# Two weight blocks of w3 loaded and turned first, and the order of all work planned again (attention and feed-forward, one core)

## The chip, the core and the metric

The kernel runs on one core of a Trainium2 chip. The metric is the device time of one execution in microseconds. A core has a matrix engine (TensorE, in the profile PE, with its weight loads as PEld), a vector engine (VectorE, DVE), a scalar engine (ScalarE, ACT), a general engine (GpSimd, POOL) and a queue for transfers (SyncE, SP). Transfers are issued from SP, ACT and POOL; the loads that also convert float32 to bfloat16 are all issued from POOL.

## The reference

```python
def _attn_ref(q, k, v, g_q, g_k):          # 8 batches, 12 heads, 448 positions, 64 values a head
    q_n, k_n = (rmsnorm(q, g_q), rmsnorm(k, g_k))
    scores = scale * np.matmul(q_n, k_n.transpose(0, 1, 3, 2))
    attn = np.exp(scores - np.max(scores, axis=-1, keepdims=True))
    attn = attn / (np.sum(attn, axis=-1, keepdims=True) + 1e-09)
    return np.matmul(attn, v)

def _moe_ref(x, w1, w2, w3, w_out):        # x is (3584, 768): the attention's heads side by side
    a = x @ w1                             # w1, w2: (768, 1024)
    b = x @ w2
    h = a * b @ w3                         # w3: (1024, 1024)
    return h @ w_out                       # w_out: (1024, 768)
```

## The kernel before, in words

**Units.** The attention is cut into 24 units: a batch and four of its twelve heads. For each unit the kernel loads q and k (L380), squares them on ACT (L477), sums the squares on DVE (L484), takes the scale from a logarithm and an exponential on ACT (L493, L496) and multiplies on DVE (L507). The scaled values are turned (transposed) to `qkT`: by PE for the first five units (L1134, in `do_turn`, with a copy from PSUM at L365 or L371), by transposing transfers on SP for the others (L579, in `send`). Seven score passes follow for a unit (`do_score`, matmuls L690); each fills two PSUM banks and is emptied by one exponential on ACT (L712). When all seven are done and `v` has landed (L420), the values follow (`start_pv`: L777 for the main part, L756 for a rest that two units share, when two units are taken together). ACT makes the reciprocal of the sums (L799, L800), DVE multiplies by it and writes `xT` (L819).

**Feed-forward.** Because `(a*b) @ w3 @ w_out` equals `(a*b) @ (w3 @ w_out)`, the kernel first computes the product of w3 and w_out once. For that w3 is loaded in eight blocks of 128 rows (`load_w3`, L455) and w_out in four quarters (`load_wout`, L461). PE turns each w3 block (`do_w3_turn`, L1156), a copy writes it to `w3T`, and pairs of passes multiply it with w_out (`w34_pair`, run by `do_pass`, matmuls L879); the result is `w34s`. Then for each batch four pairs of products with w1 and four with w2 follow (`ffn1_pair`), DVE multiplies the two (L960), and tiles of the product go through `w34s` (`ffn2_pair`), are copied from PSUM and stored (L1016). All of these matmuls are at L879; the trace tells them apart by their tiles (`w3T`, `w1s`, `w2s`, `abT`). The last tile has its own code (`do_last`, L1075).

**Halves of the array.** A pass is four matmuls of 64 rows by 64 columns that run side by side. After half of a pair's sums the two row halves exchange their banks; the instruction after the exchange waits for a small waiting instruction on SP or POOL (`hand_over`, L863), which itself waits for PE.

**The order of work.** No engine finds its order at run time. While the program is built, a planner (`Planner`) keeps a clock, one expected duration for each kind of job, and a model of the transfers, and takes one job after the other in the order of its expected times. The constants at the head of the kernel function steer it: how many pairs are open at once (`PAIRS`), by how much PE's work is put after its inputs (`MARGINS`), when scores go ahead of feed-forward passes (`STARVES`, `HUNGERS`, `FULL`), which of the score turns are given up (`AGAINST`), how late transfers land (`LATE`) and so on. Loads on POOL are issued in the order of `POOL_ORDER`, in which o is a quarter of w_out, w a block of w3, a and b a third of w1 and w2, q the two loads of a unit's q and k, and v the four loads of a unit's v. Each issue on POOL waits until the load eight places before it has landed. Where the planner sees PE idle in the first microseconds it puts matmuls without a use (`do_warm`, L1204), after fifteen larger ones at the very beginning (L1331).

Of the kernel before, what the change touches and what calls it, by code (L numbers as in the profile page):

```python
# [19 lines left out]
INF = float("inf")  # L20
# [4 lines left out]
LAG = {"ACT": 0.11, "DVE": 0.09, "SP": 0.0, "POOL": 0.0}  # L25
AHEAD = {"SP": 2.0, "POOL": 1.6}
AFTER = 0.7
LATE = 0.581
BUSY = 75.0


# [14 lines left out]
class Planner:  # L46
# [50 lines left out]
    def commit(self, job, start, engine):  # L97
# [9 lines left out]
        if job.moves is not None:  # L107
# [4 lines left out]
            def landed(t):  # L112
                self.note(job, t, engine)
                t += LATE if t > BUSY else 0.0
                ticket[0] = t
# [80 lines left out]
def kernel(  # L196
# [40 lines left out]
    psum = ctx.enter_context(tc.tile_pool(name="ps", bufs=1, space=PSUM))  # L237

    N_PE_T = 5
    QUAD = 13.0  # L240
    WARM = 15
    WARM_TO = 13.0
    WARM_N = 256
    PAIRS = (2, 3)
    MARGINS = (0.25, 0.294)
    LOWS = (2, 2)
    VALUE_BANKS = (6, 6)
    HOLD = 1
    SOONS = (0, 0)
    STARVES = (4, 5)  # L250
    HUNGERS = (0.6, 0.461)
    ONES = (0, 0)
    FULL = (0.3, 0.247)
    PARTS = ((2, 4, 6, 8), (2, 4, 6, 8), (4, 8))
    EARLY_PAIRS = 3
    AHEAD_W3 = 4
    EARLY = 4
    STOCKS = (14, 14)
    PACES = (1.7, 1.774)
    SWITCH = 55.0  # L260
    LATER = 11.735
    BY_G = 0.36
    KEYS = (1.8, 1.725)
    AGAINST = (34, 49, 79, 99, 106, 116, 117, 134, 151, 166, 172, 176, 185, 190, 197, 219, 244, 250, 265, 270, 282, 289, 301, 307, 318, 327)
    POOL_ORDER = (
        "o0 w0 w1 w2 o1 o2 o3 q1 v0 w3 w4 q2 w5 a0 v1 w6 w7 v2 a1 v3 q3 a2 b0 b1 q4 q5 b2".split()
    )
    ON_POOL = (1, 2, 3, 4, 5)
    IN_PARTS = (6, 7, 8)
    FIRST = 3.5  # L270
    THIN_FROM = 8
    THIN = 1.2
    QUIET = 0.546

    w1s = const.tile([128, CM, DFF], BF, name="w1s")
    w2s = const.tile([128, CM, DFF], BF, name="w2s")
# [45 lines left out]
    plan = Planner()  # L322

    def phase():
        return int(plan.now >= SWITCH)

    def quad(i):
        return QUAD * min(i, 6) + LATER * max(i - 6, 0)

    free, add = plan.free, plan.add  # L330
# [16 lines left out]
    w_at = {"w3": [INF] * CF, "w3T": [INF] * CF, "w_out": [INF] * 4, "w1": [INF] * NQB, "w2": [INF] * NQB}  # L347
# [120 lines left out]
    def plan_prep(i):  # L468
# [53 lines left out]
        s["red_at"] = [INF, INF]  # L522
        s["sent"] = [INF, INF]
        scaled_x = [[], []]
        pieces = ((0, 1), (1, 2)) if i == 0 else ((0, 2),)

        def reduced(t):
            def done(z):
# [47 lines left out]
            return done  # L576

        def send(t):
            nc.sync.dma_start_transpose(  # L579
                out=s["qkT"][:, t], in_=s["qks"][:, t].rearrange("p j x d -> p (j x d)")  # L580
            )
# [146 lines left out]
    def pv_size(t):  # L728
# [7 lines left out]
        if pv_one(i + 1, t):  # L736
            return 2
        if next_score[0] >= (i + 2) * NU - SOONS[phase()]:
            return 0
        if i == 1:  # L740
            return 0
        stock = sum(p.name != "w" for p in waiting)
        return 1 if stock < LOWS[phase()] or all_of(w34_at, CF) > t else 0

# [85 lines left out]


    pairs = []
    waiting = []
    running = [None]

# [21 lines left out]
    def hand_over(p, mm, t):  # L857

        at = t + 0.23
        e = "POOL"  # L860
        if max(w_at["w2"]) == INF or free["SP"] <= at and plan.moving["POOL"]:
            e = "SP"
        nop = (nc.sync if e == "SP" else nc.gpsimd).nop()  # L863
        tc.add_manual_dep(
            nop.ins, mm.ins.name, SYNC_DEP, reason="first half of the sums complete"
        )
        free[e] = max(free[e], at)
        p.gap_at = free[e] + 0.15
        p.nop = nop
# [304 lines left out]
    def next_pair(t):  # L1174
        if len(pairs) >= (EARLY_PAIRS if w_at["w_out"][3] == INF else PAIRS[phase()]):
            return None
# [17 lines left out]
    def pe_step(t):  # L1194

        took = pe_try(t, t - MARGINS[phase()])
        took = pe_try(t, t) if took is None else took
        if took is None and t < WARM_TO and idle_banks(t):
            return do_warm(single(idle_banks(t)))
# [52 lines left out]
    def pe_try(t, r):  # L1252
# [9 lines left out]
        last = HOLD and pairs and not any(p.ready() <= r for p in waiting)  # L1262
        if size == 2 and len(idle) >= VALUE_BANKS[phase()] and not last:
            return start_pv(t, 2, idle)
# [159 lines left out]
```

## Time and profile before

| what | value |
|---|---|
| median of three runs | 351.48 us (350.93 to 351.58) |
| the profiled execution's own time | 351.21 us |
| its span in the profile | 349.4 us |
| PE busy | 342.1 us, 98% of the span |
| ACT busy | 264.1 us, 76% |
| DVE busy | 203.6 us, 58% |
| granted TensorE clock | 1.0 |

The span goes from the first to the last instruction; 1.81 us of the profiled execution's time lie outside it. Matmuls are pipelined, so the busy time of PE is not the time in which it does useful work. What PE loses is read from the distance between the starts of two passes that follow each other: a pass of 448 columns after another starts 0.189 us later, one of 384 columns 0.162 us later, and what is over that is a wait or a change of the array's shape.

### The profile page before, as it was taken

The page shows a single profiled execution, that of the slowest core. Times are in us where ns is not written, and L with a number is a line of the kernel's source. Part 1 is how long each engine was busy: PE and PEld are TensorE (multiplying, and loading weights), DVE is VectorE, ACT ScalarE, POOL GpSimd, SP SyncE. Part 2 cuts the span into 40 slices and gives each one's busy share as a digit, 9 for nine tenths or more (in the row PEclk, how much of TensorE's full clock was granted, in tenths as well). Part 3 has the DMA queues.
Part 4 walks back from the last instruction along what each step waited for, and adds up shares of the span by engine and source line. Part 5 has one row for each costly group of instructions (what it writes and reads, how often), then busy time and mean ns, then how long its engine had stood idle before and what let it go on. Part 6 is the DMA issues. An engine that isn't in the chain of part 4 may idle for free.

```text
span 349.4 us, 16159 instructions
## 1 busy us (share of the span) xinstructions
PE 342.1 (98%) x7373; PEld 216.6 (62%) x7373; DVE 203.6 (58%) x292; ACT 264.1 (76%) x375; POOL 77.0 (22%) x134
## 2 busy tenths in 40 slices
PE   8999999999999999999999999999999999999995
PEld 4766756666665766556656575566565656666674
DVE  5369377988859597479657985687513421222100
ACT  4769979979998999888899997787796872222122
POOL 8366820202221403221122032204311000000000
PEclk9999999999999999999999999999999999999999
DMA  8999999587996999967999999955971013200054
GB/s 195 235 279 186 236 289 253 131 181 154 201 219 206 164 186 223 172 201 146 169 218 244 172 172 188 252 148 71 167 111 21 4 47 82 59 4 2 4 171 149
DMA packets 68488, 55.11 MB, mean 158 GB/s; under 512 B 45060, under 2 KB 62372, under 8 KB 68420
## 3 DMA queue, kind: packets, MB, share of 16 engines
q1 hardware_dynamic: 49440, 35.33, 43.5%
q0 software_dynamic: 18048, 16.92, 28.6%
q10 hardware_dynamic: 932, 1.84, 1.4%
q8 instruction: 57, 0.93, 1.1%
q14 instruction: 11, 0.09, 0.1%
HBM read 46.66 MB, written 11.01 MB: 165 GB/s over the span
## 4 chain that ended last, share of the span: by engine, by line
PE 85%; ACT 5%; DMA 3%; DVE 3%; issue 2%; POOL 2%; POOLq 0%; DVEq 0%
PE ps_all L879 62%; PE ps_all L777 11%; PE ps_all L690 9%; DMA w_outs<-in_moe_w_out_dram 3%; ACT P L712 2%; PE ps_all L756 2%; ACT sq L477 1%; DVE qks L507 1%; PE ps_all L1075 1%; POOL w_outs L461 1%; DVE xT L819 1%; POOL w3s L455 0%; PE ps_all L1156 0%; DVE ssq L484 0%; DVE abT L960 0%
## 5 line engine op out<-in xcount | busy, mean ns | idle before, releaser
L712 ACT ACTIVATE P<-ps_all 128x896 bf16<-128x896 f32 x114 | 101.0, 917 | 9.7 <-PE ps_all L690 8.6
L420 POOL DMA_DIRECT2D v_sb<-in_v_dram x96 | 57.4, 614 | 179.3 <-PE ps_all L690 107.2
L879 PE MATMUL ps_all<-xT,w2s 64*64 64x448 bf16 x1536 | 88.5, 349 | 0.1
L879 PE MATMUL ps_all<-xT,w1s 64*64 64x448 bf16 x1536 | 87.8, 349 | 0.0
L879 PE MATMUL ps_all<-w34s,abT 64*64 64x384 bf16 x1728 | 78.5, 323 | 0.0
L365 ACT ACTIVATE half<-ps_all 128x768 f32<-128x768 f32 (+1 forms) x38 | 32.6, 862 | 49.0 <-PE ps_all L879 48.8
L960 DVE TENSOR_TENSOR abT<-ps_all,half 128x896 bf16<-128x896 f32 x32 | 34.9, 1089 | 54.4 <-PE ps_all L879 52.6
L879 PEld LDWEIGHTS <-abT 64*64 64x64 bf16 x1728 | 51.6, 107 | 19.6 <-issue 0.4
L484 DVE TENSOR_REDUCE ssq<-sq 128x14 f32<-128x896 f32 (+1 forms) x50 | 51.1, 1042 | 20.2 <-ACT sq L477 20.2
L879 PEld LDWEIGHTS <-w2s 64*64 64x64 bf16 x1536 | 45.6, 107 | 26.7 <-issue 0.3
L879 PEld LDWEIGHTS <-w1s 64*64 64x64 bf16 x1536 | 45.1, 107 | 26.8
L690 PE MATMUL ps_all<-qkT 64*64 64x448 bf16 x672 | 60.3, 351 | 0.7 <-DVE qkT L371 0.3
L507 DVE TENSOR_TENSOR qks<-qk_sb,al 128x448 bf16<-128x448 f32 x96 | 54.5, 618 | 4.3 <-ACT al L496 4.1
L477 ACT ACTIVATE sq<-qk_sb 128x896 f32<-128x896 f32 (+1 forms) x50 | 45.2, 916 | 0.4 <-DMA qk_sb<-in_q_dram 0.4
L819 DVE TENSOR_TENSOR xT<-ps_all,r 128x448 bf16<-128x448 f32 x48 | 27.5, 618 | 17.1 <-ACT r L800 14.7
L690 PEld LDWEIGHTS <-qkT 64*64 64x64 bf16 x672 | 20.8, 106 | 15.0 <-issue 4.7
L879 PE MATMUL ps_all<-w_outs,w3T 64*64 64x384 bf16 x512 | 25.1, 323 | 1.2 <-DVE w3T L371 0.5
L777 PE MATMUL ps_all<-P,v_sb 128*32 128x448 bf16 x456 | 25.0, 352 | 0.0
L712 ACT ACTIVATE w_outs<-ps_all 128x896 bf16<-128x896 f32 x24 | 21.4, 916 | 4.1 <-PE ps_all L690 3.8
L777 PEld LDWEIGHTS <-v_sb 128*32 128x32 bf16 x592 | 15.8, 97 | 12.2
L712 ACT ACTIVATE Pr<-ps_all 128x896 bf16<-128x896 f32 x24 | 22.0, 917 | 0.8 <-PE ps_all L690 0.7
L879 PEld LDWEIGHTS <-w3T 64*64 64x64 bf16 x512 | 15.3, 107 | 7.6 <-SPq L863 1.1
(62 smaller groups left out, 207.0 us busy)
## 6 DMA issues: line engine op xcount, KB each, us to landing
out_dram<-half SPq DMA_DIRECT2D x48, 192.0 KB, 3.3
qk_sb<-in_q_dram SPq DMA_DIRECT2D x15, 448.0 KB, 5.7
qk_sb<-in_k_dram SPq DMA_DIRECT2D x15, 448.0 KB, 5.4
v_sb<-in_v_dram POOLq DMA_DIRECT2D x48, 64.0 KB, 4.0
v_sb<-in_v_dram POOLq DMA_DIRECT2D x48, 48.0 KB, 4.3
qk_sb<-in_q_dram POOLq DMA_DIRECT2D x5, 448.0 KB, 11.1
qk_sb<-in_k_dram POOLq DMA_DIRECT2D x5, 448.0 KB, 12.6
w3s<-in_moe_w_dram POOLq DMA_DIRECT2D x8, 256.0 KB, 6.9
```

What stands on the lines that cost most here:

```text
L365: nc.scalar.activation(out=out, in_=in_, func=AF.Copy, scale=1.0 if by is None else by)
L420: nc.gpsimd.dma_start(out=v_bufs[i % 4][p0 : p0 + HP, g::2, 0 : j1 - j0].rearrange("p h j d -> p h (j d)"), in_=src[:, g::2, j0:j1].rearra ...
L477: nc.scalar.activation(out=s["sq", t][:, x0:x1], in_=src[:, t, x0:x1], func=AF.Square)
L484: nc.vector.tensor_reduce(out=s["ssq"][:, t, x0:x1], in_=s["sq", t][:, x0:x1], axis=AX, op=ADD)
L507: nc.vector.tensor_tensor(out=s["qks"][:, t, :, x], in0=src[:, t, x], in1=s["alpha"][:, t, x].unsqueeze(2).broadcast_to([NP, NJ, D]), op=MULT,
L690: nc.tensor.matmul(out=sc[HP * c : HP * c + HP, u, 0:S].rearrange("p (j s) -> p j s", j=NJ), lhsT=qkT[u * D : (u + 1) * D, 1, j, cols], rh ...
L712: lambda: nc.scalar.activation(out=dst, in_=sc[:, :, 0:S], func=AF.Exp),
L756: nc.tensor.matmul(out=ps_all[hd * HALF : (hd + 1) * HALF, banks[x], 0:S], lhsT=(v_bufs[(i + x) % 4][g : g + HP, hd, NF, kind - 1 :: 2] if ...
L777: nc.tensor.matmul(out=ps_all[hd * HALF : (hd + 1) * HALF, z, 0:S], lhsT=value_weights(i, hd, j, kind), rhs=s["P"][:, hd, j, :] if j < NF ...
L819: lambda: nc.vector.tensor_tensor(out=xT[b][:, 2 * m + kind - 1, :], in0=ps, in1=s["r"], op=MULT),
L879: mm = nc.tensor.matmul(out=ps_all[64 * h : 64 * h + 64, p.bank + z, 0 : p.n], lhsT=lhsT[64 * r : 64 * r + 64, 64 * h : 64 * h + 64], rhs= ...
L960: nc.vector.tensor_tensor(out=abT[bp][:, f0 : f0 + 2, odd * S : (odd + 1) * S], in0=ps_all[:, z : z + 2, 0:S], in1=a_sb[b, f0], op=MULT,)
```

## The change

The loads on POOL begin with two blocks of w3, and only then the first quarter of w_out; the four loads of the first unit's values go ahead of the last quarter of w_out; the third unit's values go behind the second third of w1. Nearly all of the planner's constants get other values. Two rules are new: the planner keeps the time of the last transposing transfer that was sent (`sent_at`), and `hand_over` takes SP only when 3.0 us (`LONGEST_SEND`) have gone by since; and the cut of a unit's squares into two pieces hangs on a constant `SPLIT`, with the value that it had. Because each engine's order comes from the planner, the new constants move work on every engine. The numbers of all the arithmetic instructions together are unchanged; a few copies from PSUM move between ACT and DVE, and 16 instead of 22 small matmuls without a use are emitted.

```diff
-LATE = 0.581
+LATE = 0.359
...
-    QUAD = 13.0
+    QUAD = 13.317
     WARM = 15
-    WARM_TO = 13.0
+    WARM_TO = 13.868
     WARM_N = 256
-    PAIRS = (2, 3)
-    MARGINS = (0.25, 0.294)
-    LOWS = (2, 2)
-    VALUE_BANKS = (6, 6)
+    PAIRS = (2, 2)
+    MARGINS = (0.271, 0.289)
+    LOWS = (0, 3)
+    VALUE_BANKS = (6, 5)
     HOLD = 1
-    SOONS = (0, 0)
-    STARVES = (4, 5)
-    HUNGERS = (0.6, 0.461)
+    SOONS = (2, 3)
+    STARVES = (5, 4)
+    HUNGERS = (0.645, 1.406)
     ONES = (0, 0)
-    FULL = (0.3, 0.247)
+    FULL = (0.486, 0.3)
...
-    STOCKS = (14, 14)
-    PACES = (1.7, 1.774)
+    STOCKS = (17, 13)
+    PACES = (1.157, 1.173)
     SWITCH = 55.0
-    LATER = 11.735
+    LONGEST_SEND = 3.0
+    SPLIT = 1
+    LATER = 13.429
     BY_G = 0.36
-    KEYS = (1.8, 1.725)
-    AGAINST = (34, 49, 79, 99, 106, 116, 117, 134, 151, 166, 172, 176, 185, 190, 197, 219, 244, 250, 265, 270, 282, 289, 301, 307, 318, 327)
+    KEYS = (1.8, 1.636)
+    AGAINST = (74, 167, 174, 210, 228, 247, 290, 327)
     POOL_ORDER = (
-        "o0 w0 w1 w2 o1 o2 o3 q1 v0 w3 w4 q2 w5 a0 v1 w6 w7 v2 a1 v3 q3 a2 b0 b1 q4 q5 b2".split()
+        "w0 w1 o0 w2 o1 o2 v0 o3 q1 w3 w4 q2 w5 a0 v1 w6 w7 a1 v2 v3 q3 a2 b0 b1 q4 q5 b2".split()
     )
...
-    THIN_FROM = 8
-    THIN = 1.2
-    QUIET = 0.546
+    THIN_FROM = 9
+    THIN = 1.964
+    QUIET = 0.746
...
-        pieces = ((0, 1), (1, 2)) if i == 0 else ((0, 2),)
+        pieces = ((0, 1), (1, 2)) if i < SPLIT else ((0, 2),)
...
         def send(t):
+            sent_at[0] = plan.now
...
-        if max(w_at["w2"]) == INF or free["SP"] <= at and plan.moving["POOL"]:
+        if max(w_at["w2"]) == INF or (
+            max(free["SP"], sent_at[0] + LONGEST_SEND) <= at and plan.moving["POOL"]
+        ):
             e = "SP"
```

More of the change, by code (lines that the diff above doesn't have):

```diff
@@ L832 @@
     pairs = []
+    sent_at = [0.0]
     waiting = []
```

## The prediction

> **What bounds the kernel now.** I read the page's busy times and its chain first, then the waits of PE, then PE's timeline around each wait, and last the distances between the starts of passes.
>
> ```profile
> PE 342.1 (98%) x7373; PEld 216.6 (62%) x7373; DVE 203.6 (58%) x292; ACT 264.1 (76%) x375; POOL 77.0 (22%) x134
> ...
> PE   8999999999999999999999999999999999999995
> ...
> PE 85%; ACT 5%; DMA 3%; DVE 3%; issue 2%; POOL 2%; POOLq 0%; DVEq 0%
> ```
>
> PE is busy in every slice and holds 85% of the chain, so the end is set by PE: its useful work plus what it loses. In the table of stretches ACT is busy over 9.1 of each 10 us from 20 to 50 us, so in that stage ACT hands PE its work just in time. What PE waited for:
>
> ```profile
> PE ps_all L879 <- DVE w3T L371: 0.5, 1, 0.5
> PE ps_all L879 <- DMA w_outs<-in_moe_w_out_dram: 0.4, 1, 0.4
> PE ps_all L690 <- DVE qkT L371: 0.3, 1, 0.3
> PE ps_all L690 <- DVE abT L960: 0.3, 1, 0.3
> PE ps_all L690 <- ACT Pr L712: 0.2, 1, 0.2
> ```
>
> These are few, and a modelled end hides part of each, so the loss is taken from starts. In PE's timeline:
>
> ```profile
> 18.08 2.15 PE L879 MATMUL ps_all<-w_outs,w3T 64*64 64x384 bf16 x48 [0.43 <-DMA w_outs<-in_moe_w_out_dram]
> ...
> 27.14 0.84 PE L879 MATMUL ps_all<-w_outs,w3T 64*64 64x384 bf16 x16 [0.51 <-DVE w3T L371]
> ...
> 51.85 0.38 PE L690 MATMUL ps_all<-qkT 64*64 64x448 bf16 x4 [0.31 <-DVE qkT L371]
> ...
> 116.35 0.38 PE L690 MATMUL ps_all<-qkT 64*64 64x448 bf16 x4 [0.17 <-ACT Pr L712]
> 117.00 0.38 PE L690 MATMUL ps_all<-qkT 64*64 64x448 bf16 x4 [0.27 <-DVE abT L960]
> ```
>
> By starts these are 0.63 (the last quarter of w_out), 0.57 (a w3 block's copy), 0.48 (a copy of qkT), 0.34 and 0.46 us. The smaller ones over 0.12 us: 0.29 at 13.39, 0.30 at 21.62, 0.22 at 33.53, 0.22 at 61.75, 0.23 at 69.39, 0.13 at 73.29, 0.13 at 124.38.
>
> **The ledger.** From its first turn (8.42 us) PE's useful passes, priced by start distances (scores, values and w1/w2 passes 0.189, w_out and w34 passes 0.162, turns 0.39 and 0.45, the last tile 0.165), are 326.1 us less the last pass's own 0.165, and 49 changes of the array's shape at 0.103 are 5.0: 330.95. The last pass starts at 344.95, so 14.0 us are lost: 8.4 before the first turn, 1.0 in nine small fillers between turns, 4.6 in waits. The loss stands at 11.35 when w34's fourth block starts (27.1), 11.5 at 50, 12.3 at 73, 12.5 at 103, 13.4 at 124, 14.0 at the end. After 124 us there is nothing left to win. Behind the last pass 4.45 us of copies and stores end the span.
>
> **What the Trainium skill says.** "TensorE: Matmul & The Clock Gate", section Back-to-back issue gap, puts warm issues N/2.4 + 2.5 ns apart: 189 ns for 448 columns, 162 for 384; the trace has 0.189 and 0.162. "TensorEngine Tiling (Array Packing)", Key Properties: a change of tiling mode drains TensorE; here the last w34 pass before `do_last` is followed after 0.263 instead of 0.162, hence 0.10 for a change. "DMA: Bandwidth & Descriptors", Issuing engines are not separate DMA queues: all transfers share the same engines, so putting one load forward puts others back. The trace agrees: POOL's early loads land one after the other, a w3 block (256 KB written) 1.25 us behind the load before it, a quarter of w_out (384 KB) 1.88.
>
> **Part 1: w0 and w1 ahead of o0.** Times of landing are the last semaphore increments of each load: o0 8.03, w0 9.28, w1 10.54, w2 11.80, o1 13.67, o2 15.55, o3 18.03, q1 19.29, k1 20.92, the last of v0 21.94, w3 23.19, w4 24.50. In the new order w0 lands at about 8.03 - 1.88 + 1.25 = 7.4, w1 8.65, o0 10.5, w2, o1 and o2 as before. PE's new order is w3 turn, six fillers, w3 turn, q turn, three fillers, k turn, seven fillers, two w34 passes, the first two scores. The two w3 turns end at 9.15, so the q turn moves from 8.42 to 9.15, the k turn from 9.59 to 9.87; both copies of qkT now stand on DVE (0.62 each), the w3 copies on ACT (1.01). The first score comes at 11.46 instead of 11.18, with two w34 passes (0.32) already done: **0.0**. Then PE waits about 0.2 for a bank (first exponential 11.9 to 12.8), reaches o1 after it has landed, and o2 at 16.2 after 15.55.
>
> **Part 2: v0 ahead of o3.** v0's four loads (0.3 each) then land by about 17.5, o3 at 18.03 + 1.2 = 19.3, q1 20.6, k1 22.1; w3 to w7 as before, since the bytes ahead of them are the same. On POOL's queue v0's issues (0.6 each) move ahead; o3's goes back from 6.1 to about 10.6 and q1's from 6.8 to 11.9, since each waits for the load eight places before (o0, w2), but five to eight loads are always under way, so the engines have no gap. PE has w34 passes to 18.3, then the first unit's values (twelve passes, 2.3 us with the changes; the seventh exponential is done at 18.3), and takes o3 up at 20.8, 1.5 us after landing. The wait of 0.63 goes, and the 0.30 at 21.62. What is late next: the second unit. k1 at 22.1, its square on ACT to 23.1, sum to 24.2 (1.08), two multiplications on DVE to 25.4, so the q turn that PE reaches at 25.05 starts at 25.5: 0.45 lost. The w3 copies stand behind those multiplications on DVE, the fourth block's passes start at 26.15. At that place of the new order (15.5 us of work done) the loss is 10.65 against 11.35: **-0.7**.
>
> **Part 3: more changes of shape.** The new PE order has 54 changes, not 49; all work is otherwise equal, 326.1: 5 x 0.103 = **+0.5**, on the path.
>
> **Part 4: units 1 to 4, 27 to 75 us.** The first score of unit 1 moves back from 16.4 to 19.9 us of work, that is from 27.8 to about 30.6, but the values of units 1 and 2 only from 34.0 to 34.3. ACT has fourteen exponentials at 0.80 apart (11.2), one w34 copy (0.7) and a square (0.84) from 31.0: ready at 43.8 against PE's 45.0. Before the first scores of unit 3 the new order puts twelve feed-forward passes and more, where the old one ran into the 0.48 wait for a copy; the turns at 61.75 and the waits at 69.39 and 73.29 (0.58) likewise stand elsewhere. Of 1.06 us I take 0.2 to stay: **-0.85**. The bounds: all of it gone (-1.06), or as much put in elsewhere (+0.5).
>
> **Part 5: the rest.** The waits at 116 come where four scores follow each other with no other pass ready; the new order has such a row of four at the same unit: 0. From 125 on there is no wait to remove, and ACT has 0.6 to 3.3 of each 20 us free up to 240: 0. `LONGEST_SEND`: the waits for a hand-over are
>
> ```profile
> PEld L879 <- SPq L863: 1.1, 5, 0.5
> ```
>
> all five with `w3T` as weights, before a transposing transfer is sent. The built kernel has 42 of its 106 hand-overs on SP, where it had 35: 0, between -0.1 and +0.5 (a waiting instruction moved to POOL stands behind value loads of 0.6 us). `LATE` alone moves nothing that the trace prices. Six fewer fillers are in the ledger. Copies that change between ACT and DVE are hidden beside PE. The tail is the same instruction by instruction: 4.45.
>
> **Sum:** 0.0 - 0.7 + 0.5 - 0.85 = -1.05. The profiled execution (351.21: span 349.4 and 1.81 around it) would become 350.2; it was 0.27 under the median of 351.48, so I say **350.4**.
>
> **Rivals.** *It stays where it is* (the early gain is given back: k1 lands 0.5 later than I think, and unit 3 and 4 stall as before): -0.7 + 0.5 + 0.5 - 0.2 = +0.1, 351.6. For it: ACT over 91% busy in that stage, so any delay goes on. Against it: the 0.63 and 0.57 waits have named causes that the order removes.
>
> *The exponentials of units 1 and 2 become last* (slower). They start 2.8 us later than now. PE has only fourteen w34 passes (2.3 us) after the last score, and no feed-forward pass may start before the first batch's six xT pieces are written. The slack is 45.0 - 43.8 = 1.2 us; it decides once q1, k1 or the copies are over 1.2 + 1.05 = 2.3 us later than worked out. A slip of 3.5 gives 3.5 - 1.2 - 1.05 = +1.3: 352.8. For it: a late load is what the timeline shows at 18.08 already. Against it: the bytes ahead of w3 are unchanged.
>
> *The plan holds better than I credit* (all waits from 27 to 124 us go, 2.1, the q turn's 0.45 too): -0.7 - 0.45 + 0.5 - 2.1 = -2.75: 348.7.
>
> *It does not do what it says*: w0 lands late as the first load in the queue, after PE's first turn stands waiting; each us costs up to one us of the q turn. Bound: w0 at 8.03 as o0 did, +0.6, that is 351.0.
>
> **Chances.** My forecast 0.42, better still 0.18, about unchanged 0.25, slower 0.15. A measurement of this kernel tells about 0.2%, 0.7 us, from no change. Faster by more than that: 0.61; within: 0.20; slower: 0.19. The range reaches from the better case to most of the slower one: 348.7 to 352.4. For the forecast alone it is 349.7 to 350.9.
>
> **What would show it.** Right: no PE wait on w_outs, first values on PE at about 18.4, fourth w34 block by 26.2, no wait on qkT at 51, the loss at most 11.5 when the values of units 3 and 4 start (about 72.5, now 73.3). Wrong: PE waiting for w3s at 7 us beyond 0.7; a stall ahead of the values at 45; new waits behind L863's counterpart on POOL; a row of scores with ACT as releaser after 125 us.

## The result: 353.76 us, 0.7% slower, where 350.4 was forecast

| | before | after |
|---|---|---|
| median (lowest to highest) | 351.48 us (350.93 to 352.2, nine runs) | 353.76 us (352.1 to 355.56, nine runs) |
| after over before, 95% interval | | 1.0066 [1.0044, 1.0088] |
| profiled execution: own time, span | 351.21, 349.4 us | 353.76, 352.0 us |
| start of the last pass | 344.95 us | 347.55 us |

The page of the changed kernel: busy time by engine, PE in 40 slices, and the shares of the chain that ended last.

```profile
PE 342.7 (97%) x7367; PEld 219.1 (62%) x7367; DVE 198.9 (57%) x288; ACT 265.3 (75%) x379; POOL 76.8 (22%) x134
...
PE   7999999999999899999999999999999999999995
...
PE 87%; DMA 7%; DVE 1%; ACT 1%; SPq 1%; issue 1%; POOL 0%; POOLq 0%; DVEq 0%
```

PE still sets the end, but ACT's part of the chain (5% before) has become DMA's (3% before, 7% now), and beside the first and the last slice there is one in which PE is not full, the fourteenth, at 114 to 123 us. What PE waited for (us in total, times, longest), the largest first:

```profile
PE ps_all L1162 <- DMA w3s<-in_moe_w_dram: 1.4, 1, 1.4
PE ps_all L693 <- DVE half L373: 0.9, 1, 0.9
PE ps_all L780 <- issue: 0.6, 1, 0.6
PE ps_all L885 <- DVE abT L966: 0.4, 1, 0.4
PE ps_all L1162 <- ACT P L715: 0.3, 1, 0.3
```

None of the five names is in the list of before. The changed kernel's lines stand 2 to 6 lower in the file (L879 is L885, L690 L693, L777 L780, L484 L486, L515 L517, L371 L373, L960 L966). In PE's timeline these are:

```profile
8.61 0.62 PE L1162 MATMUL ps_all<-ident,w3s 128*128 128x128 bf16 x8 [1.41 <-DMA w3s<-in_moe_w_dram]
...
19.54 0.75 PE L780 MATMUL ps_all<-P,ones 128*32 128x448 bf16 x12
...
22.00 3.44 PE L885 MATMUL ps_all<-w_outs,w3T 64*64 64x384 bf16 x80
...
50.14 0.55 PE L780 MATMUL ps_all<-P,v_sb 128*32 128x448 bf16 x6 [0.58 <-issue]
...
118.08 0.76 PE L693 MATMUL ps_all<-qkT 64*64 64x448 bf16 x12 [0.92 <-DVE half L373]
119.28 1.33 PE L885 MATMUL ps_all<-w34s,abT 64*64 64x384 bf16 x28 [0.43 <-DVE abT L966]
...
228.51 0.38 PE L693 MATMUL ps_all<-qkT 64*64 64x448 bf16 x4 [0.24 <-ACT P L715]
```

By starts the last four stops are 0.75, 1.11, 0.63 and 0.42 us. The early waits of before are gone as planned: PE takes up the last quarter of w_out at 22.00 without a wait. But a sign that the prediction had named for being wrong is there: PE waits 1.41 us for w3s. And a score pass after 125 us waits for ACT (228.51).

The last pass starts 2.6 us later than before. The prediction's ledger (loss: start of a pass less the useful work before it) says where they lie:

| useful work done, us | loss before | loss after | difference |
|---|---|---|---|
| 28 | 11.46 | 11.70 | +0.24 |
| 77 | 12.43 | 12.98 | +0.55 |
| 100 | 12.49 | 13.12 | +0.63 |
| 109 | 13.31 | 14.88 | +1.57 |
| 185 | 13.60 | 15.23 | +1.63 |
| 234 | 13.73 | 15.83 | +2.10 |
| end | 14.00 | 16.08 | +2.08 |

To the 2.08 come 0.52 for the five more changes of the array's shape, which count as useful work here (5 at the prediction's price of 0.103): 2.60, as the starts of the last pass say.

**The stop at 118 us, read backwards.** PE's scores wait for the copy `half`. DVE's timeline shows why that copy is late:

```profile
115.43 0.61 DVE L517 TENSOR_SCALAR qkT<-qkT,g_col 128x896 bf16<-128x896 bf16 x1 [0.88 <-DMA qkT<-qks]
115.96 1.07 DVE L486 TENSOR_REDUCE ssq<-sq 128x14 f32<-128x896 f32 x1
116.95 1.07 DVE L373 CAST half<-ps_all 128x896 bf16<-128x896 f32 x1
118.13 1.09 DVE L966 TENSOR_TENSOR abT<-ps_all,half 128x896 bf16<-128x896 f32 x1
```

DVE stands 0.88 us at the multiplication by g, because its transposed q has not landed (sent at 109.44, landed at 115.41), and the sum of squares, the copy and the product queue behind it. Such a wait alone need not cost PE anything. DVE's waits for transposed q, of before and then of after, over the whole run:

```profile
DVE qkT L515 <- DMA qkT<-qks: 6.5, 5, 3.1
```

```profile
DVE qkT L517 <- DMA qkT<-qks: 2.7, 4, 0.9
```

Before stands there longer than after, once for 3.1 us at 246.6, and yet PE has no stop over 0.13 us from 118 us on. A late landing costs time where work that PE needs stands behind it in the engine's order. At 228 us that is so on ACT, with k in place of the transposed q:

```profile
226.70 0.95 ACT L479 ACTIVATE sq<-qk_sb 128x896 f32<-128x896 f32 x1 [0.47 <-DMA qk_sb<-in_k_dram]
```

ACT's waits for q and k, of before and then of after:

```profile
ACT sq L477 <- DMA qk_sb<-in_q_dram: 0.4, 1, 0.4
```

```profile
ACT sq L479 <- DMA qk_sb<-in_q_dram: 2.0, 3, 1.0
ACT sq L479 <- DMA qk_sb<-in_k_dram: 0.9, 3, 0.5
```

From 0.4 to 2.9 us. The 0.4 of before and 0.8 of the 2.9 are the first unit's, at 4 to 5 us. The rest is new: 1.2 for unit 4 at 54 and 55 us, and 0.9 for units 11, 22 and 23 at 110.8, 216.2 and 226.7 us. For these later units the two timelines differ in room: from the last multiplication that reads a buffer of q and k to the first square of the unit that gets the buffer next there are 18.8 us on average in before (units 9 to 23), and 11.9 in after. Within it the load has to be issued and moved (medians of 5.1 to 5.7 us from issue to landing on both pages).

### The profile page after: what moved, and what is told of

Same layout as the page of the kernel before. It is cut to its first block, busy times and chain, and to the rows that moved or that the text cites. A ratio compares the mean times of both kernels' runs of the same rounds, so it can differ in the third digit from the quotient of the medians.

```text
span 352.0 us, 16147 instructions
## 1 busy us (share of the span) xinstructions
PE 342.7 (97%) x7367; PEld 219.1 (62%) x7367; DVE 198.9 (57%) x288; ACT 265.3 (75%) x379; POOL 76.8 (22%) x134
## 4 chain that ended last, share of the span: by engine, by line
PE 87%; DMA 7%; DVE 1%; ACT 1%; SPq 1%; issue 1%; POOL 0%; POOLq 0%; DVEq 0%
PE ps_all L885 62%; PE ps_all L780 11%; PE ps_all L693 8%; PE ps_all L759 2%; DMA w3s<-in_moe_w_dram 2%; DMA qkT<-qks 2%; DMA qk_sb<-in_k_dram 2%; DMA qk_sb<-in_q_dram 1%; PE ps_all L1140 1%; PE ps_all L1162 1%; PE ps_all L1081 1%; SPq L1022 1%; DVE half L373 1%; ACT sq L479 1%; PE ps_all L1210 1%
## 5 line engine op out<-in xcount | busy, mean ns | idle before, releaser
L715 ACT ACTIVATE P<-ps_all 128x896 bf16<-128x896 f32 x114 | 99.7, 919 | 9.4 <-PE ps_all L693 8.9
L885 PE MATMUL ps_all<-xT,w2s 64*64 64x448 bf16 x1536 | 88.0, 349 | 0.0
L885 PE MATMUL ps_all<-xT,w1s 64*64 64x448 bf16 x1536 | 87.9, 349 | 0.0
L885 PE MATMUL ps_all<-w34s,abT 64*64 64x384 bf16 x1728 | 80.2, 323 | 0.4 <-DVE abT L966 0.4
L367 ACT ACTIVATE half<-ps_all 128x896 bf16<-128x896 f32 (+1 forms) x42 | 36.4, 869 | 47.9 <-PE ps_all L885 47.9
L966 DVE TENSOR_TENSOR abT<-ps_all,half 128x896 bf16<-128x896 f32 x32 | 34.8, 1089 | 57.2 <-PE ps_all L885 54.6
L885 PEld LDWEIGHTS <-abT 64*64 64x64 bf16 x1728 | 51.6, 107 | 20.5 <-issue 0.7
L885 PEld LDWEIGHTS <-w2s 64*64 64x64 bf16 x1536 | 46.7, 107 | 25.6 <-issue 0.4
L486 DVE TENSOR_REDUCE ssq<-sq 128x14 f32<-128x896 f32 (+1 forms) x50 | 51.2, 1041 | 19.4 <-ACT sq L479 19.4
L885 PEld LDWEIGHTS <-w1s 64*64 64x64 bf16 x1536 | 46.4, 107 | 25.0
L693 PE MATMUL ps_all<-qkT 64*64 64x448 bf16 x672 | 60.0, 352 | 1.2 <-DVE half L373 0.9
L693 PEld LDWEIGHTS <-qkT 64*64 64x64 bf16 x672 | 21.9, 106 | 15.1 <-issue 5.8
L780 PE MATMUL ps_all<-P,v_sb 128*32 128x448 bf16 x456 | 25.4, 353 | 0.6 <-issue 0.6
L885 PE MATMUL ps_all<-w_outs,w3T 64*64 64x384 bf16 x512 | 25.1, 324 | 0.0
L780 PEld LDWEIGHTS <-v_sb 128*32 128x32 bf16 x592 | 15.9, 97 | 13.1 <-issue 1.2
L885 PEld LDWEIGHTS <-w3T 64*64 64x64 bf16 x512 | 15.0, 107 | 6.0 <-issue 0.6
```

The lines of the kernel that those rows point to most:

```text
L367: nc.scalar.activation(out=out, in_=in_, func=AF.Copy, scale=1.0 if by is None else by)
L486: nc.vector.tensor_reduce(out=s["ssq"][:, t, x0:x1], in_=s["sq", t][:, x0:x1], axis=AX, op=ADD)
L693: nc.tensor.matmul(out=sc[HP * c : HP * c + HP, u, 0:S].rearrange("p (j s) -> p j s", j=NJ), lhsT=qkT[u * D : (u + 1) * D, 1, j, cols], rh ...
L715: lambda: nc.scalar.activation(out=dst, in_=sc[:, :, 0:S], func=AF.Exp),
L780: nc.tensor.matmul(out=ps_all[hd * HALF : (hd + 1) * HALF, z, 0:S], lhsT=value_weights(i, hd, j, kind), rhs=s["P"][:, hd, j, :] if j < NF ...
L885: mm = nc.tensor.matmul(out=ps_all[64 * h : 64 * h + 64, p.bank + z, 0 : p.n], lhsT=lhsT[64 * r : 64 * r + 64, 64 * h : 64 * h + 64], rhs= ...
```

## The experiments

Each time is a median, beside the ratio to the kernel before on the same chip. "Row" is what the stops at 115 to 119.7 us, in the row of scores, add up to; losses are by useful work, as above. A profile is of one execution: those of a_again, a_memset and a_noq3 took 0.5, 1.1 and 0.95 us more than their kernels' medians, those of a_noqk and a_noqk3 0.6 and 0.3 less.

### Is it the kernel or the run?

> The changed kernel once more, unchanged, for a second profile of it. Theory A (the loss has fixed places): the first turn of a w3 block starts at 8.6 us again, PE stands still for about 0.75 us near 50 us with no releaser shown, and for 1.1 + 0.6 us near 118 us; the ratio to the kernel before is 1.005 to 1.008. Theory B (the places differ from run to run: where an instruction fetch or a load happens to be late): the total stays near 2.3 us but at least one of the three places is gone or moved by this profile, as the spread of its nine times (352.1 to 355.6) against 350.9 to 352.2 of the kernel before suggests.

The changed kernel as it is: **354.18 us, 1.0073 [1.0049, 1.0096]**. The stops stand where they stood: 0.79 at 49.9 (again without a releaser), row 1.59, and at 229.46 now 1.23 instead of 0.42:

```profile
227.66 0.95 ACT L479 ACTIVATE sq<-qk_sb 128x896 f32<-128x896 f32 x1 [0.99 <-DMA qk_sb<-in_k_dram]
```

So the places belong to the order, and the size of a stop behind a landing varies from run to run: ACT's waits for units 9 to 23 add up to 2.5 us here, where they were 0.9. The first turn starts at 8.37.

### The start alone

```diff
-        for t_sb in v_bufs:                       # ahead of all loads on POOL
-            nc.gpsimd.memset(t_sb[:, :, NF, :], 0.0)
...
 def load_w3(c):
...
+        if c == 1:                                # behind the second load of w3
+            for t_sb in v_bufs:
+                nc.gpsimd.memset(t_sb[:, :, NF, :], 0.0)
```

> The changed kernel with the four memsets of v_sb on POOL (1.06 us) put behind the issue of the two w3 blocks; nothing else moves on any engine. Theory 1 (the wait for the first block counts one for one): the first block is issued at 1.3 instead of 2.3 us, lands 1 us earlier, the first turn starts at about 7.6, and the total falls by 0.7 to 1.0 us. Theory 2 (the early delay is absorbed: PE's stretch up to 40 us has slack behind other waits): the first turn starts earlier, but the loss at 40 us of work falls by under 0.3 us and the total by under 0.3. Theory 3 (the first load lands at a time set by other traffic): the landing does not move.

**353.77 us, 1.0067 [1.0042, 1.0091]**. The first turn comes at 7.67, 0.94 earlier than in the first profile, and at 28 us of work the loss is 10.69, 1.0 less. At 185 us it is 15.15 against 15.23: all given back in this execution. ACT shows one of the places, unit 4's k (its timeline, then PE's; the lines of this kernel stand 4 lower):

```profile
55.01 0.95 ACT L483 ACTIVATE sq<-qk_sb 128x896 f32<-128x896 f32 x1 [1.13 <-DMA qk_sb<-in_k_dram]
```

```profile
56.82 1.90 PE L889 MATMUL ps_all<-xT,w1s 64*64 64x448 bf16 x36 [0.70 <-ACT P L719]
```

The same edit in the kernel before, where the memsets go behind the first load, o0:

> The kernel before with the same four memsets put behind the issue of its first load, the first quarter of w_out; nothing else moves. Loads are in a row, so all weights land up to 1 us earlier. Theory 1 (the wait at 18.08 for the last quarter of w_out is one for one): that wait of 0.63 goes and the total falls by 0.4 to 0.7 us. Theory 2 (what PE does not wait for there it waits for at 21.6 and 27.1): the total falls by under 0.2 us. If the landing of the first load is set by other traffic, nothing moves.

**352.09 us, 1.0013 [1.0001, 1.0026]**. The first load is issued at 1.43 instead of 2.26 us, but the first of the sixteen increments of a semaphore by which it reports its landing comes at 6.78 (6.98 in before) and the last at 8.96 (8.03), and PE's first turn at 9.13 (8.42). An earlier issue did not bring an earlier landing, so a_memset's early start is not shown to be due to it either. Over nine profiles whose order up to 28 us is that of the changed kernel the first turn lies between 7.04 and 8.61 us and the loss at 28 us between 10.14 and 11.70, 10.9 on average without the moved memsets; five with the order of before and its memsets in place have 11.26 to 11.46. On average over these profiles the change does gain at the start, 0.5 us. The profile of the result happened to be the worst of the nine.

### One constant or one list at a time

```diff
-LATE = 0.359                 # a_late: after with before's value
+LATE = 0.581
```

> The changed kernel with LATE back at 0.581; PE's order is the same up to the stall at 118 us and differs from there on. Theory L (with 0.359 the planner puts jobs that wait for a landing too early: at 115 us DVE stands 0.9 us for a transposed qkT with the copies that free PSUM banks queued behind it): the 1.7 us at 118 us fall to 0.8 or less, and the total by 0.8 to 1.2 us, to about 352.7. Theory T (the transfers themselves are late because more of them run together in the new order): the stall stays at about 1.7 us, and the total within 0.3 us of 353.8.

**354.63 us, 1.0116 [1.0073, 1.0159]**. The order is the same up to 118 us: row 1.61, no less than in the other profiles of the changed kernel; from there new stops, the largest 0.64 at 221.7. LATE alone doesn't repair it. (Two of the six executions took about 358 us, which is why the ratio lies above that of the medians.)

```diff
-LATE = 0.581                 # b_late: before with after's value
+LATE = 0.359
```

> The kernel before with LATE 0.359 instead of 0.581 alone (the planner counts on landings 0.22 us earlier after 75 us); the order is the same up to about 89 us. Theory L (the smaller allowance makes instructions stand for landings): ACT stands 1.5 us or more for q and k, the time is 352.3 to 353.5, with stops behind landings. Theory N: 352.5 to 354.5 with stops of other kinds. If neither: 351.5.

**354.10 us, 1.0063 [1.0041, 1.0085]**. ACT stands 0.3 us for q and k, all of it for the first unit, so theory L falls; the new stops are 0.59 at 118.3, behind a transpose, and 0.81 at 134.3, behind an exponential.

```diff
-    THIN_FROM = 9            # a_thin: after with before's values
-    THIN = 1.964
+    THIN_FROM = 8
+    THIN = 1.2
```

> The changed kernel with the two constants that hold back the loads of q and k on SP as in the kernel before (THIN_FROM 8, THIN 1.2). The order stays the same up to about 96 us and is planned anew from there. Theory T with the held loads as its source: the loads of 104 to 105 us no longer stand ahead of the transposes of 109 us, the stop at 118 falls under 0.5 us, and unless the rest of the new order is worse by chance the time is 351.8 to 352.6. Rival (what matters is the luck of an order that is made anew, not this constant): stops of 1 us and more at other places, 353.0 to 354.5.

**355.10 us, 1.0091 [1.0070, 1.0112]**. The row falls to 0.78, but there are 1.05 at 95.4, behind the landing of a transpose, and 0.76 at 170.5, behind a copy on ACT: stops at other places, as the rival said, and a time above its range.

```diff
-    THIN_FROM = 8            # b_thin: before with after's values
-    THIN = 1.2
+    THIN_FROM = 9
+    THIN = 1.964
```

> The kernel before with two of the changed constants alone: THIN_FROM 9 and THIN 1.964, so that loads of q and k on SP are sent while more of what SP moves is still under way. The order is the same up to about 80 us and is planned anew from there. Theory S (this rule is what brings the landings of q and k too close to their squares): ACT stands 2 us or more for q and k instead of 0.4, PE stops once or twice by 0.5 to 1.2 us after 90 us, the time is 352.8 to 354.0. Theory N (any order made anew costs that much, whichever constant is touched): also 352.5 to 354.5, but the stops show no landing of q or k ahead of them, and leaving these loads out gains nothing.

**355.02 us, 1.0091 [1.0067, 1.0115]**, 1.0 us above the range of theory S and 0.5 above that of N. ACT does stand for loads now (0.7 of these waits is the first unit's), and PE stops by 0.68 at 229.2 behind the first of these:

```profile
ACT sq L477 <- DMA qk_sb<-in_k_dram: 2.0, 1, 2.0
ACT sq L477 <- DMA qk_sb<-in_q_dram: 1.0, 2, 0.7
```

> The same, with the loads of q and k for units 9 to 23 left out (these units use the values of the unit three before); no other instruction moves. Theory T or S: the stops after 90 us fall to what before has (0.8), the time comes down by 1 us or more, to 351.3 to 352.2. Theory N: no change, within 0.4 us of the kernel that has the loads.

**354.27 us, 1.0069 [1.0050, 1.0088]**: of the 3.6 us that b_thin is over before, the loads of q and k account for 0.75, and the two intervals overlap. Neither theory is right by itself. The stops that remain (0.78 at 137.8 behind a copy on DVE, 0.62 at 196.0 behind an exponential) are of that order itself.

```diff
-        "o0 w0 w1 w2 o1 o2 o3 q1 v0 w3 ... v2 a1 v3 ...".split()     # b_order: before with after's list
+        "w0 w1 o0 w2 o1 o2 v0 o3 q1 w3 ... a1 v2 v3 ...".split()
```

> The kernel before with the changed order of the loads on POOL alone (two blocks of w3 first, first values ahead of the last quarter of w_out), all else planned anew with the constants of before. If the early part of the change is worth what was forecast (0.6 to 0.7 us by 28 us of useful work), the loss there is 10.7 to 11.0 instead of 11.46; if early gains are handed back at landings that come at their own time, the end is 351.5 or later whatever the start. Expected: start gained, end 352.0 to 354.0. Rival (the start is kept): 350.5 to 351.0.

**355.55 us, 1.0110 [1.0091, 1.0129]**. The part of the change that its name tells of, alone: at 28 us of work the loss is 10.27, 1.2 less than before, more than was hoped (one profile; the average above is 0.5). Then PE stops at 48.8 without a releaser:

```profile
48.84 0.56 PE L777 MATMUL ps_all<-P,v_sb 128*32 128x448 bf16 x6 [0.71 <-issue]
```

by 0.88, and again by 0.33, 0.64 and 0.17 at 73.7 to 75.2 and by 1.19 at 219.0, where four exponentials and a copy follow each other on ACT. The loss at the end is 17.10. So this profile gains at the start, and the order made for it loses 4.3 us more than before does from there on.

All five orders that were made anew for one part of the change or with one part undone lose 2.6 to 4.1 us to the kernel before. Why an order made anew stops PE more often was not settled; landings are only a part of it. The room for the loads of units 9 to 23, and ACT's waits for them, in the orders that have all loads:

| order | room on average, us | ACT's waits for these loads, us |
|---|---|---|
| before | 18.8 | 0 |
| b_late | 16.7 | 0 |
| b_order | 16.1 | 0 |
| a_thin | 15.9 | 0.6 |
| after, a_again | 11.9, 12.0 | 0.9, 2.5 |
| a_late | 11.8 | 1.9 |
| b_thin | 11.6 | 2.3 |

Each row is one profile (after's row two). Where the room is small ACT stands for these loads, and where it is large hardly or not at all. But b_late, b_order and a_thin, with room and next to no such waits, lose 2.6 to 4.1 us all the same.

### Loads left out: the stop at 50 us

```diff
     def load_qk(i, which, eng, x0=0, x1=2):
+        if i == 3:
+            return None
```

> The changed kernel without the two loads of unit 3's q and k on POOL (issued ahead of the first third of w1; unit 3 computes with unit 0's values). No other instruction moves. Theory I (the stop of 0.5 to 0.8 us at 50 us, which shows no releaser, is PE's own instruction stream, fetched late while the weights of w1 and w2 and the q loads fill the transfers): with 0.9 MB less the stop falls under 0.25 us and the time by 0.3 to 0.5, to 353.3 to 353.5. Theory P (the stop belongs to the order on PE, a weight load behind a wait): it stays at 0.5 or more, the time stays at 353.8.

**353.68 us, 1.0047 [1.0025, 1.0069]**. The two loads are issued at 37.7 and 38.4 us in the changed kernel, ahead of the last third of w1. The stop at 50 us is gone (0.00; the next pass still waits 0.13 for DVE), which speaks for theory I. The trace has packets of instructions, here those of after's page (queue: packets, MB, share of the 16 DMA engines):

```profile
q8 instruction: 57, 0.93, 1.1%
```

They are 16 KB each and take some 0.96 us; PE's 14734 instructions over 57 packets are some 258 to a packet, so they are taken to be PE's. How many PE instructions (twice the matmuls) had begun when the sixth of them started, beside the size of the stop:

| kernels | instructions begun | stop, us |
|---|---|---|
| b_thin, b_thin_noqk, before, b_noqk, b_memset | 1594 to 1610 | 0 |
| a_noq3 | 1622 | 0 |
| a_noqk3, a_swap, a_late, b_late | 1638 to 1642 | 0.15 to 0.33 |
| a_noqk, a_memset | 1646 | 0.39, 0.45 |
| a_thin | 1654 | 0.61 |
| after, a_again, a_swap2, b_order | 1662 to 1664 | 0.74 to 0.88 |

PE begins eight instructions (four weight loads, four matmuls) in 0.189 us, so each pass of delay in the fetch costs about a pass. Over 17 profiles the stop goes with the start of that packet: what stops PE is its own instruction stream, fetched late. What makes it late is less clear. Without unit 3's loads the count is 1622 and 1638; in the eight profiles that have them and the changed kernel's order up to there it is 1638 to 1662.

The median hardly fell. By the ratios it is 0.7 to 0.9 us below the changed kernel, with intervals that overlap, and the thirteen executions spread from 351.55 to 355.84, six of them under 352.7. In the profiled one (354.63) what was won was lost again: the loss is 10.43 at 60 us of work (after 12.77) and 16.89 at the end (16.08). PE's timeline, and ACT's ahead of the second line:

```profile
140.60 1.14 PE L885 MATMUL ps_all<-xT,w1s 64*64 64x448 bf16 x20 [0.98 <-DVE half L373]
...
227.67 0.38 PE L693 MATMUL ps_all<-qkT 64*64 64x448 bf16 x4 [1.43 <-ACT P L715]
```

```profile
225.86 0.95 ACT L479 ACTIVATE sq<-qk_sb 128x896 f32<-128x896 f32 x1 [1.81 <-DMA qk_sb<-in_q_dram]
```

These two stops are 1.30 and 1.78 us; ahead of the first DVE had stood 2.27 us for a transposed q. A third, 0.93 at 94.7, is behind a transpose itself. All three are at landings.

### Loads left out: units 9 to 23

```diff
     def load_qk(i, which, eng, x0=0, x1=2):
+        if i >= 9:
+            return None
```

> The changed kernel without the loads of q and k for units 9 to 23, which all stand on SP; these units compute with the values of the unit three before. No other instruction moves. Theory T (the stops at 118 and 228 us come from transfers that land after the instruction in ACT's or DVE's order that needs them, with copies and exponentials queued behind it): the transposing transfers of 109 to 111 us land some 2.5 us after their issue instead of 5.9, by_g no longer stands, the stop of 1.7 us at 118 falls under 0.5 and the one at 228 under 0.1; the time falls by 1.3 to 2.2 us, to 351.6 to 352.5. Theory O (the order itself overloads ACT or DVE there, whatever the transfers do): the stop at 118 keeps over 1.2 us, the time stays within 0.5 of 353.8.

**352.47 us, 1.0024 [1.0015, 1.0033]**. The stop at 228 is gone, the row falls to 0.96 (0.84 without a wait of 0.12), and the transposes of 108.8 and 110.2 us land after 2.8 and 2.7 us. The stop did not fall under 0.5 as expected: 0.22 and 0.62 are left, the second behind an exponential. DVE no longer stands ahead of the sum of squares and the copy:

```profile
113.38 0.44 DVE L517 TENSOR_SCALAR qkT<-qkT,g_col 128x896 bf16<-128x896 bf16 x1
```

A wait that is left is unit 4's q, whose loads stand on POOL; PE stops for 0.47 at 56.2 after it:

```profile
53.22 0.95 ACT L479 ACTIVATE sq<-qk_sb 128x896 f32<-128x896 f32 x1 [1.95 <-DMA qk_sb<-in_q_dram]
```

> The kernel before with the same loads left out (q and k of units 9 to 23; the values of the unit three before are used), no other instruction moves. Theory T: before had room ahead of most of these landings, so that it gains less than the changed kernel, 0 to 0.8 us (the 0.8 at 116 to 117 us is all that could be due to them): 350.7 to 351.5, and the distance between the two kernels shrinks from 2.3 us to 0.5 to 1.2. Theory O: nothing moves, 351.5, and the distance stays at 2.3.

**351.57 us, 0.9996 [0.9979, 1.0014]**, the same as before; row 0.80. The distance between the two kernels shrinks from 2.3 to 0.9 us.

> The changed kernel without the loads of q and k for unit 3 and for units 9 to 23 (these units use the values of the unit three before). No other instruction moves. If early time is handed back because later loads of q and k land at times of their own, then with these gone the early gain stays: no stop at 50 us, loss at 28 us of useful work 10.1 to 10.9, at the end 12.2 to 13.3, time 351.0 to 351.8. Rival (it is handed back for another reason, in the order of ACT and DVE): the same time as with units 9 to 23 alone left out, 352.5.

Both edits together: **351.30 us, 0.9990 [0.9972, 1.0007]**. Loss 10.46 at 28 us, 12.55 at 185, 12.96 at the end, with one stop over 0.25 us from there on:

```profile
116.40 0.38 PE L693 MATMUL ps_all<-qkT 64*64 64x448 bf16 x4 [0.43 <-ACT P L715]
```

| changed kernel | q, k of units 9 to 23 loaded | left out |
|---|---|---|
| unit 3's loaded | 353.76, 354.18 | 352.47 |
| unit 3's left out | 353.68 | 351.30 |

By medians, leaving out unit 3's loads gains 0.1 to 0.5 us while the later loads are there (0.7 to 0.9 by the ratios, which compare on one chip), and 1.2 us when they are not. This difference is not clear of the noise. Some 0.7 of the 1.2 are the wait for unit 4's q with its stop at 56.2, which is gone, and the stop at 50, which falls from 0.39 to 0.15. That **time won early is taken back at later landings of q and k** is what the profiles of the changed kernel's order show, each of one execution:

| loss at | after | a_again | a_memset | a_noq3 | a_swap | a_swap2 | a_noqk | a_noqk3 |
|---|---|---|---|---|---|---|---|---|
| 28 us | 11.70 | 11.39 | 10.69 | 10.14 | 11.45 | 10.70 | 10.52 | 10.46 |
| 185 us | 15.23 | 15.16 | 15.15 | 14.38 | 14.89 | 14.31 | 13.35 | 12.55 |
| 234 us | 15.83 | 16.78 | 16.89 | 16.63 | 16.23 | 16.40 | 13.51 | 12.70 |

With the later loads in, the loss at 234 us lies between 15.8 and 16.9 whatever it was at 28; the two that came to 185 us with the least (14.4 and 14.3) lost the most from there to 234 (2.25 and 2.1). Without them 0.15 are lost there. It need not happen in every execution: six of a_noq3's thirteen were about as fast as a_noqk.

### One instruction moved

```diff
 DVE, from 115 us:
  L517 qkT<-qkT,g_col
- L486 ssq<-sq
  L373 half<-ps_all
  L966 abT<-ps_all,half
+ L486 ssq<-sq
```

> The changed kernel with one instruction moved: on DVE the sum of squares of unit 12's q (L486) goes behind the copy (L373) and the product (L966) that follow it, at 116 us. Every other engine's order is the same. Theory Q (the changed kernel's extra stop in the row of scores at 118 us comes from by_g, which stands 0.9 us for its transposed q, with this sum of 1.07 us between it and the copy that frees the banks): the stop of 1.7 us falls to 0.7 to 0.9, what the other orders show there, and the time by 0.6 to 1.0, to 352.8 to 353.3. Rival G (time won is handed back at the next landing, as in the kernel without unit 3's loads): the stop falls as much, a later one behind a landing of q or k grows, the time stays at 353.5 to 354.1.

**353.90 us, 1.0068 [1.0045, 1.0091]**. DVE's timeline:

```profile
115.27 0.63 DVE L517 TENSOR_SCALAR qkT<-qkT,g_col 128x896 bf16<-128x896 bf16 x1 [1.15 <-DMA qkT<-qks]
115.82 1.07 DVE L373 CAST half<-ps_all 128x896 bf16<-128x896 f32 x1
117.00 1.09 DVE L966 TENSOR_TENSOR abT<-ps_all,half 128x896 bf16<-128x896 f32 x1
118.01 1.08 DVE L486 TENSOR_REDUCE ssq<-sq 128x14 f32<-128x896 f32 x1
```

DVE stands even longer for the transposed q (1.15), and yet the copy comes 1.1 us earlier and the row falls from between 1.6 and 1.7 us to 0.93, what the other orders have. So the cause of the extra stop at 118 is shown: the late transpose (gone in a_noqk) together with the sum of squares in front of the copy (moved here). The rival was right about the time: 0.53 us at 141.1 behind DVE and 1.17 at 228.9 behind this take it back:

```profile
227.11 0.95 ACT L479 ACTIVATE sq<-qk_sb 128x896 f32<-128x896 f32 x1 [1.03 <-DMA qk_sb<-in_k_dram]
```

```diff
 ACT, from 225 us, besides:
- L479 sq<-qk_sb          (unit 23's k)
  L715 P<-ps_all
+ L479 sq<-qk_sb
```

> The same, and on ACT the square of unit 23's k (L479), which stands for its landing at 226.7 us, goes behind the next exponential. Theory Q: the stop at 228.5 us (0.4 to 1.8 us in the runs so far) falls to 0.1 or nothing too, and the time by 0.3 to 1.0 against the kernel with the first move alone: 352.2 to 353.0. Rival G: no gain over the first move.

**354.64 us, 1.0077 [1.0048, 1.0107]**. Row 0.95; the stop there is now 0.54 at 226.2 (the square of the same unit's q stands 0.73 us for its landing ahead of it), and 1.37 at 231.0, where PE waits for an exponential that now stands behind the moved square's chain. Moving one instruction aside only moved the stop. Whether loads that come earlier would help was not run.

None of these kernels that does the whole work beats the kernel before.

## Why the prediction was wrong, step by step

**Transfers, the view that was left out.** The prediction read the waits, the chain and ACT's busy time, but never the last two columns of the table of stretches (the DMA engines' share and GB/s); of the engines it says only that they "have no gap" in the first 25 us. Rows of 50 us, from 100 us on, of before, of after, and of the changed kernel without the q and k loads of unit 3 and of units 9 to 23 (a_noqk3):

```profile
100.00:150.00 50.00, 49.56 (x1100) 31.14 (x1096) 36.51 (x53) 46.60 (x68) 10.57 (x18) 1.00 0.99 195
150.00:200.00 50.00, 50.00 (x1104) 30.72 (x1100) 39.72 (x57) 45.75 (x65) 9.51 (x16) 1.00 0.89 189
```

```profile
100.00:150.00 50.00, 48.64 (x1076) 31.15 (x1072) 39.74 (x57) 46.50 (x69) 11.53 (x20) 1.00 1.07 212
150.00:200.00 50.00, 50.00 (x1100) 30.32 (x1092) 36.07 (x52) 47.81 (x70) 10.10 (x17) 1.00 0.94 195
```

```profile
100.00:150.00 50.00, 49.52 (x1092) 31.75 (x1088) 39.99 (x58) 47.06 (x70) 9.62 (x17) 1.00 0.71 110
150.00:200.00 50.00, 50.00 (x1100) 30.55 (x1096) 35.15 (x50) 47.93 (x70) 11.65 (x20) 1.00 0.52 83
```

The last two numbers are to be read: the time of the packets is 0.89 to 1.07 of what the 16 engines have, in both kernels (0.88 to 1.07 from the start to 200 us), and 0.5 to 0.7 without these loads. It can pass 1 since packets overlap, so a share near 1 is a sign that transfers are full, and no proof. With the loads left out transposes landed sooner: at 109 us after 2.8 us instead of 6.0, in the median after 3.5 (a_noqk) instead of 4.5. Whether this comes from the fullness or from the order in SP's queue wasn't separated. Nor does fullness alone set the two kernels apart: before is nearly as full, and gains nothing when the same loads go (b_noqk).

The Trainium skill, "DMA: Bandwidth & Descriptors", Issuing engines are not separate DMA queues, says that transfers issued by ACT, SP and POOL end up on the same 16 engines and interleave there. It doesn't speak of packets of instructions; the profile's page counts them with the others. That PE's packet came a little sooner without two loads on POOL (1622 and 1638) agrees with that, but the counts touch those with the loads. And "Trainium Architecture — The Big Picture", Inside one NeuronCore, says that each engine has an instruction stream of its own and meets the others only at semaphores; the copy that stood behind a late multiplication (115.43 above) is what that costs, 0.9 us.

By the ledger of the profile the forecast of -1.05 became +2.60: parts 1 and 2 gave +0.24 for -0.7, part 4 gave +0.31 for -0.85, what part 5 covers, from 77 us of work on, gave +1.53 for 0, and part 3 came as forecast. The steps, one by one:

- **Part 1, w0 at 7.4 us: failed in size.** The first turn stood until 8.61 in the profile, and from 7.04 to 8.61 over all profiles of this order. The landing was worked out from the distance between loads, 7.4 us; the first load's last increment came at 8.56 in the profile of the result and between 6.99 and 8.56 in the nine. "w0 lands late" was a rival, priced at +0.6.
- **Part 2, -0.7: right in mechanism, a little large.** The waits for the last quarter of w_out went and the values came ahead of it, at 19.54 instead of 18.4 in the profile, because all of it starts late there. On average the gain is 0.5, in the profile of the result it is a loss of 0.24.
- **Part 3, +0.5: as forecast.** The trace has 54 changes of shape; at 0.103 each the five more are 0.52. No run measures them alone.
- **Part 4, 27 to 75 us, -0.85: failed.** From 28 to 77 us of work after loses 1.28 and before 0.97: +0.31. The step counted which waits of before would go, and let nothing new come but 0.2. The stop at 50 us, with no releaser (0.75), is something that before doesn't show at all. Why the packet comes later in this order stays open.
- **Part 5, the row of four scores, 0: failed**, +0.94 (0.63 to 1.57 in the table). The floor of such a row was seen rightly: 0.8 to 1.2 in all other orders. That DVE might enter it late, behind a transpose, was left out of the sum. "From 125 on there is no wait to remove" was true, and no reason that none would be added: +0.47 at 228.
- **LONGEST_SEND, 0: nothing speaks against it.** PEld's wait for a hand-over went from 1.1 to 0.2, in an order that is new as a whole; no run changes this rule alone:

```profile
PEld L885 <- SPq L869: 0.2, 1, 0.2
```

- **The rivals.** The slower one (exponentials of units 1 and 2 become last) came near in size, 352.8, by a mechanism that didn't happen: no wait stands ahead of the values at 45 us. "The early gain is given back" named the right kind of event, but priced at 351.6, with nothing beyond the start lost.
- **The general step.** The sum priced an order by the waits of the old order that it removes. Five orders made anew all lost 2.6 to 4.1 us to the kernel before, so in these cases the waits that a new order brought by itself were worth more than those that the change removed, and zero was a wrong centre for them. The price of a pass (0.189, 0.162), on which the ledger rests, held: it is the trace's own distance between passes in a row, while the formula that the prediction cites for it is given in the Trainium skill ("TensorE: Matmul & The Clock Gate", Back-to-back issue gap) for a single matmul by itself.

Of the 2.3 us, 1.3 to 1.5 are due to the loads of q and k from unit 9 on (353.76 to 352.47 by medians, 1.0066 to 1.0024 by ratios): that is shown by leaving them out, with before as the control. The rest is an estimate from the ledger: 0.5 for the changes of shape and 0.75 for the stop at 50 us, less 0.5 won at the start on average.

## What to carry to other kernels

Before pricing a reordering, compare for each load the room (buffer free to first use) with issue to landing; a new order that uses the data sooner, with the same buffers, can turn hidden loads into waits. Then look at what stands behind the first user in its engine's order: here a wait of 3.1 us on DVE cost PE nothing, and one of 0.9 us in front of a copy that frees banks cost it about as much. Read the DMA share by stretches too, even where every page line says TensorE: time won ahead of a landing can be lost at it. And where an order is a planner's, don't price its constants by the stops they remove: an order made anew has its own.

## What the runs showed of the hardware that was not expected

- Instructions come in packets of 16 KB while the kernel runs, 57 of them, counted among the traffic of the 16 DMA engines. Where the sixth of them started late by the count of PE's instructions (1638 to 1664 instead of up to 1622), PE stopped, by 0.15 to 0.88 us, with "issue" and no releaser.
- POOL's first load, a w3 block, had its first increment at 6.04 to 6.32 us in all runs, whether issued at 1.44 or at 2.26, and a quarter of w_out at 6.68 to 6.98, whether at 1.43 or 2.26. From the first to the last increment it took 0.6 to 2.3 us, differing from run to run.
- A transposing transfer took 2.8 us from issue to landing with the q and k loads of units 9 to 23 left out and 6.0 with them, at the same place of the same order.
